# Reordering the first five microseconds of a convolution and ReGLU kernel: which queue fetches what, and in what order the band is built

## The chip, the cores and the metric

The kernel runs on one core of one Trainium2 chip. The metric is the device time of one execution in microseconds (us), with the median of several runs as the kernel's time. Five engines work side by side, each through its own queue of instructions in order: TensorE (PE in the profile; PEld is its weight load), VectorE (DVE), ScalarE (ACT), GpSimd (POOL) and SyncE (SP), which here only issues transfers.

## The reference

A causal convolution of seven taps along the sequence, one softmax-normalised set of taps for each of eight heads, followed by a feed-forward layer with a ReLU gate:

```python
# x: (8, 4096, 192), weight: (8, 7); 24 channels per head
w = softmax(weight, axis=-1)
x_pad = concat([zeros(8, 6, 192), x], axis=1)
conv[b, s, h, g] = sum_k w[h, k] * x_pad[b, s + k, h, g]
t = conv.reshape(32768, 192)
out = (maximum(t @ w_gate, 0) * (t @ w_val)) @ w_out   # 192 -> 1536 -> 192, float32
```

## The kernel before

The eight sequences are taken as two streams of four, `st` 0 and 1, which sit on the two halves of the partitions. The work goes in units of 1024 tokens of both streams, and a unit in two windows of 512. For a window, `gate_val` (L515) multiplies the convolved tokens `xc` with the gate and value weights, in twelve slices of 128 hidden columns; ScalarE applies the ReLU (L526), VectorE multiplies (L527). After two windows `project` multiplies with `w_out` (L544) and the results go out. There are sixteen units, and in each but the last, which ends a little differently, TensorE does the same 288 matmuls of L515 and 384 narrower ones of L544.

From the second unit on, the convolution is done on VectorE, ScalarE and GpSimd, one unit ahead, beside TensorE's work. The first unit has nobody ahead of it, so TensorE does its convolution itself, as a matmul with a band matrix: `band(h)` holds the seven taps of head h along its diagonals, and `conv_dense` (L366) multiplies 110 rows of x, each row a token, with it. That gives `xc` with channels on partitions, as L515 wants it. `conv_dense(0, c)` does it for each of three groups of 64 channels, c = 0, 1, 2, forty matmuls each, over five blocks `jj` of 104 tokens and the two streams. c = 0 uses heads 0, 1 and 2; c = 1 uses heads 2 to 5, and c = 2 heads 5 to 7.

The start, up to the first L515, is this:

- **x.** SyncE fetches blocks 1 to 4 of the first stream as fp32 into `room` (L120), and block 0 of both streams (L136); ScalarE casts the former to fp16 (L312), VectorE the latter (L327). Blocks 1 to 4 of the second stream are fetched by GpSimd's queue (L125), which casts on the way, straight to `x_h`. The small tensor `weight` goes first on SyncE's queue (L99).
- **The taps.** VectorE takes the maximum of the taps (L247), ScalarE exponentiates them (L250), VectorE sums, takes the reciprocal and scales (L254 to L257). A small matmul (L268) brings the taps of all heads to the partitions where they are wanted, in `spread`.
- **The mask and the band.** GpSimd writes a mask `spaced` (L126); VectorE sums it over the taps in two ways (L234, called twice), for `same` and `places`. The product of `spread` and `same` (L278) is `diag`; fourteen matmuls (L288) shift it into place in PSUM, seven for heads 0 to 3 (`bps`), seven for heads 4 to 7 (`spread`, second bank). Copies (L321) bring the band to fp16: VectorE heads 0 to 2, later head 3; ScalarE heads 4 to 7.
- **The weights.** GpSimd's queue fetches gate and value weights in slices (L168). Each is doubled to the upper partitions (L175); VectorE does so for the first two slices.
- **Warm-up.** `warm_up` (L152) issues matmuls on constants whose results nobody reads, in four places.

The order on each engine is the program's order, written out by hand; waits between engines are added from the data that instructions share. In `conv_dense(0, 0)` the blocks 1 to 4 of the first stream come first, then those of the second, and block 0 last:

```python
late = (1, 2, 3, 4, 0)
both = [(jj, (0, 1)) for jj in late]
if g == 0 and c == 0:
    both = [(jj, (st,)) for st in range(2) for jj in late[0:4]] + both[4:]
```

Of the kernel before, what the change touches and what calls it, by code (L numbers as in the profile page):

```python
# [8 lines left out]
FP = mybir.dt.float32  # L9
F16 = mybir.dt.float16  # L10
ACTF = mybir.ActivationFunctionType
ALU = mybir.AluOpType
# [3 lines left out]
def kernel(  # L16
# [12 lines left out]
    nc = tc.nc  # L29

    B, S, D = x.shape
    H, KW = weight.shape
    G = D // H
    DFF = moe_w_gate.shape[1]
    PAD = KW - 1
    NB = B // 2
# [5 lines left out]
    SUB = 112  # L42
    VECTOR = [(0, 5), (1, 5), (2, 5), (0, 6), (2, 1)]
    FOR_POOL = [(1, 6), (2, 6)]
    GSUB = 5
    DSUB = 104
# [12 lines left out]
    const = ctx.enter_context(tc.tile_pool(name="const", bufs=1))  # L59
# [33 lines left out]
    xts = {}  # L93
    ROWS0 = DSUB + PAD
    GAP = 12
    SEG = 16
    NSEG = SUB // SEG
    wr = const.tile([H, KW], FP)
    nc.sync.dma_start(out=wr[:], in_=weight)  # L99
    room = apool.tile([128, KW, NCH, LPOOL], FP, name="prods")  # L100

    def stage(p0, rows, st, n_st, jj, n):
        at = room[p0 : p0 + rows, 0, 0, 0:1]
        dims = [[D * GSUB, n_st], [D, n], [1, D]]
        return bass.AP(
            tensor=at.tensor,
            offset=at.offset + D * (GSUB * st + jj),
            ap=[at.ap[0]] + [d for d in dims if d[1] > 1],
        )

    xts[0] = xpool.tile([128, GSUB, 2, D], F16, name="x_h")

    def body(st):
        return bass.AP(
            tensor=x.tensor,
            offset=x.offset + (NB * st * S + DSUB - PAD) * D,
            ap=[[D, SUB], [DSUB * D, GSUB - 1], [1, D]],
        )

    nc.sync.dma_start(out=stage(0, SUB, 0, 1, 1, GSUB - 1), in_=body(0))  # L120
    ones = const.tile([128, SUB], FP)
    nc.vector.memset(ones[:], 1.0)
    spaced = const.tile([SUB, KW, SEG + 2 * GAP], FP)
    nc.gpsimd.memset(spaced[:], 0.0)
    nc.gpsimd.dma_start(out=xts[0][0:SUB, 1:GSUB, 1, :], in_=body(1))  # L125
    nc.gpsimd.affine_select(  # L126
        out=spaced[:, :, GAP : GAP + SEG],
        in_=ones[0:SUB, 0 : KW * SEG].rearrange("p (k s) -> p k s", k=KW),
# [3 lines left out]
        base=0,  # L132
        channel_multiplier=1,
    )
    nc.vector.memset(stage(0, 32, 0, 2, 0, 1), 0.0)
    nc.sync.dma_start(  # L136
        out=stage(PAD, DSUB, 0, 2, 0, 1),
        in_=bass.AP(
            tensor=x.tensor, offset=x.offset, ap=[[D, DSUB], [NB * S * D, 2], [1, D]]
        ),  # L140
# [4 lines left out]
    places = const.tile([SUB, 2 * SUB], F16)  # L145
# [4 lines left out]
    def warm_up(*widths):  # L150
        for n, w in enumerate(widths):
            nc.tensor.matmul(  # L152
                out=warm[:, n % 2, 0:w], lhsT=busy[:, 0:128], rhs=busy[:, 0:w], start=True, stop=True
            )

    warm_up(512, 512, 512, 512, 512, 512, 128)

# [13 lines left out]
    def both_halves(copy, s, dst):  # L173
        cols = slice(CUTS[s], CUTS[s + 1])
        copy(out=dst[64:128, :, cols], in_=dst[0:64, :, cols])  # L175
# [56 lines left out]
    def summed(out, step, n, at):  # L232
        with nc.allow_low_precision("one of the terms is not zero"):
            nc.vector.tensor_reduce(  # L234
                out=out,
                in_=bass.AP(
                    tensor=some.tensor,
                    offset=some.offset + at,
                    ap=[some.ap[0], [1, n], [step, KW]],
                ),  # L240
                axis=mybir.AxisListType.X,
                op=ALU.add,
            )

    pitch_k = SEG + 2 * GAP
    mx = const.tile([H, 1], FP)
    nc.vector.tensor_reduce(  # L247
        out=mx[:], in_=wr[:], axis=mybir.AxisListType.X, op=ALU.max, negate=True
# [9 lines left out]
        out=over[:],  # L258
        in0=spaced[0:H, 0, GAP : GAP + H],
# [1 line left out]
        scalar2=None,  # L261
        op0=ALU.mult,
    )
    same = const.tile([SUB, SEG], FP)
    summed(same[:], pitch_k, SEG, GAP)
    summed(places[:, SUB - SEG : SUB - SEG + SEG + KW - 1], pitch_k - 1, SEG + KW - 1, GAP)
    spread = psum.tile([128, 2, 512], FP, name="ps")
    nc.tensor.matmul(  # L268
        out=spread[0:SUB, 0, 0:H],
# [2 lines left out]
        start=True,  # L272
        stop=True,
    )
    warm_up(512)
    diag = const.tile([SUB, H, SEG], F16)
    with nc.allow_low_precision("products with one and zero"):
        nc.vector.tensor_tensor(  # L278
            out=diag[:],
            in0=spread[0:SUB, 0, 0:H].unsqueeze(2).to_broadcast([SUB, H, SEG]),  # L280
            in1=same[:].unsqueeze(1).to_broadcast([SUB, H, SEG]),
            op=ALU.mult,
        )
    bps = psum.tile([128, 2, 512], FP, name="ps")
    HB = H // 2
    for a in range(2):
        for b in range(NSEG):
            nc.tensor.matmul(  # L288
                out=(bps, spread)[a][:, a, HB * SEG * b : HB * SEG * (b + 1)],
                lhsT=places[:, SUB - SEG * (b + 1) : SUB - SEG * (b + 1) + 128],  # L290
                rhs=diag[:, HB * a : HB * (a + 1), :].rearrange("p h s -> p (h s)"),
                start=True,
# [1 line left out]
                skip_group_check=True,  # L294
            )

    warm_up(512, 128)

    taps = const.tile([H, KW], FP)
    nc.scalar.activation(taps[:], ex[:, 0:KW, 0], ACTF.Copy, scale=sm[:])  # L300
# [1 line left out]
    for h in range(H):  # L302
        r = G * h
        while r < G * (h + 1):
            c, n = r // 64, min(64 - r % 64, G * (h + 1) - r)
            nc.sync.dma_start(
                out=tap[r % 64 : r % 64 + n, c, :],
                in_=taps[h : h + 1, :].unsqueeze(1).to_broadcast([1, n, KW]),
            )
            r += n  # L310

    nc.scalar.copy(out=xts[0][0:ROWS0, 1:GSUB, 0, :], in_=stage(0, ROWS0, 0, 1, 1, GSUB - 1))  # L312
    bands = {}

    def fill_band(a, heads, copy):
        lo, n = heads[0] - HB * a, len(heads)
        part = const.tile([128, n, SUB], F16, name=f"band{heads[0]}")
        for i, h in enumerate(heads):
            bands[h] = part[0 : SUB + PAD, i, :]
        from_ = (bps, spread)[a][:, a, 0 : HB * SUB]  # L320
        copy(  # L321
            out=part[:].rearrange("p h (b s) -> p h b s", s=SEG),
            in_=from_.rearrange("p (b h s) -> p h b s", h=HB, s=SEG)[:, lo : lo + n],
        )

    fill_band(0, [0, 1, 2], nc.vector.tensor_copy)
    nc.vector.tensor_copy(out=xts[0][0:ROWS0, 0, :, :], in_=stage(0, ROWS0, 0, 2, 0, 1))  # L327
    fill_band(0, [3], nc.vector.tensor_copy)
    fill_band(1, [4, 5, 6, 7], nc.scalar.copy)

    def band(h):
        return bands[h]
# [8 lines left out]
    def conv_dense(g, c):  # L341


        xt = xts[g]
        if g == 0 and c == 0:
            xc[0] = xcpool.tile([128, NCH, UNIT], F16, name="xc")
            both_halves(nc.vector.tensor_copy, 0, Wg)
            both_halves(nc.vector.tensor_copy, 0, Wv)
        t0 = GROUPS[g][1][0]
        rows = ROWS0  # L350
        ps = psum.tile([128, 2, 512], FP, name="ps")
        late = (1, 2, 3, 4, 0)
        both = [(jj, (0, 1)) for jj in late]
        if g == 0 and c == 0:
            both = [(jj, (st,)) for st in range(2) for jj in late[0:4]] + both[4:]
        for jj, sts in both:
            col = DSUB * jj
            n = min(DSUB, WIN - col)
            for second in range(2):
                for st in sts:  # L360
                    for k2 in range(2):
                        k = 2 * c + k2
                        h0, h1 = 32 * k // G, (32 * k + 31) // G
                        h, m = (h0, G * h1 - 32 * k) if second else (h1, 32)
                        p0 = 64 * st + 32 * k2
                        nc.tensor.matmul(  # L366
                            out=ps[p0 : p0 + m, 0, col : col + n],
                            lhsT=xt[0:rows, jj, st, 32 * k : 32 * k + m],
                            rhs=band(h)[0:rows, 0:n],
                            start=True,  # L370
                            stop=True,
                            tile_position=(0, p0),
                            skip_group_check=True,
                        )
        copy = nc.vector.tensor_copy if c == 1 else nc.scalar.copy
        copy(out=xc[0][:, c, t0 : t0 + WIN], in_=ps[:, 0, :])
# [250 lines left out]
    for c in range(NCH):  # L627
        conv_dense(0, c)
# [81 lines left out]
```

## Time and profile before

| What | us |
|---|---|
| Median of 3 runs | 767.44 (767.3 to 769.09) |
| Profiled execution | 767.38 |
| Its span, first to last instruction | 765.40 |
| TensorE busy | 760.6 (99% of the span) |
| VectorE, ScalarE, GpSimd busy | 705.6, 600.8, 377.4 |
| First matmul of L366 | at 5.50 |
| First matmul of L515 | at 7.41 |

The span is what the trace shows; the execution's own time is 1.98 us longer. A line of the timeline gives the start in the span, the length from the first start to the last end, the engine, the line of the program, the operation, what it writes and reads, and how many instructions are merged into it; in brackets stands the idle time before it and what ended that. SPq and ACTq are transfers being issued by SyncE and ScalarE. A line of the windows gives, for a stretch, its length, busy time and number of instructions of PE, PEld, DVE, ACT and POOL, then the granted clock, the share of the DMA engines' time that was busy (overlapping packets can bring it over 1) and GB/s.

### The profile page before, as it was taken

To read this page: it belongs to the slowest core of one execution; us is meant where nothing else is said; L and a number is where in the kernel's file an instruction comes from. 1 tells how busy PE (TensorE), PEld (TensorE's weight loads), DVE (VectorE), ACT (ScalarE), POOL (GpSimd) and SP (SyncE) were. 2 spreads that over 40 slices of the span, in tenths; PEclk is the share of its full clock that TensorE was granted. 3 is DMA by queue.
4 is the path that set the end of the run, shared out by engine and by line. 5 is a ranking of instruction groups with operands and counts; after the bars stand their busy time and mean duration, and the time that the engine had idled before them with its cause. 6 is when DMAs were issued, how large, how long until landed. Compare 5 with 4: busy or idle time off the path is not lost.

```text
span 765.4 us, 25193 instructions
## 1 busy us (share of the span) xinstructions
PE 760.6 (99%) x10978; PEld 501.0 (65%) x10978; DVE 705.6 (92%) x763; ACT 600.8 (78%) x733; POOL 377.4 (49%) x242
## 2 busy tenths in 40 slices
PE   9999999999999999999999999999999999999998
PEld 4594674947649476584855848567494674947657
DVE  7998999999999999999999999999999999999891
ACT  6788887878878787887878878788787887875581
POOL 8419448093571926729175390853909347090000
PEclk9999999999999999999999999999999999999999
DMA  9979037290452805529173271823719034220202
GB/s 135 104 119 144 12 95 81 64 114 16 98 67 81 99 23 108 47 85 94 31 112 39 85 93 44 113 22 92 86 47 124 11 99 58 65 48 22 64 1 85
DMA packets 131396, 56.03 MB, mean 73 GB/s; under 512 B 96325, under 2 KB 131285, under 8 KB 131285
## 3 DMA queue, kind: packets, MB, share of 16 engines
q1 hardware_dynamic: 90661, 38.82, 24.0%
q0 software_dynamic: 40480, 15.50, 20.7%
q8 instruction: 86, 1.41, 0.8%
q14 instruction: 25, 0.20, 0.1%
q10 hardware_dynamic: 144, 0.10, 0.0%
HBM read 31.49 MB, written 25.17 MB: 74 GB/s over the span
## 4 chain that ended last, share of the span: by engine, by line
PE 99%; DMA 0%; ACT 0%; SPq 0%; issue 0%
PE ps L515 65%; PE ps L544 33%; PE ps L591 1%; PE ps L366 0%; DMA prods<-in_x_dram 0%; PE ps L387 0%; ACT x_h L312 0%; SPq L99 0%; ACT acc L570 0%
## 5 line engine op out<-in xcount | busy, mean ns | idle before, releaser
L527 DVE TENSOR_TENSOR hT<-gr,ps 128x1024 f16<-128x1024 f16 (+1 forms) x386 | 469.1, 1216 | 36.9 <-ACT gr L526 10.0
L526 ACT ACTIVATE gr<-ps 128x1024 f16<-128x1024 f32 (+1 forms) x386 | 393.3, 1020 | 102.0 <-PE ps L515 100.1
L467 POOL TENSOR_TENSOR prods<-prods 128x1344 f32<-128x1344 f32 x70 | 212.3, 3033 | 289.1 <-DVE prods L463 285.7
L515 PE MATMUL ps<-xc,Wg 64*128 64x512 f16 x2304 | 311.9, 376 | 0.0
L515 PE MATMUL ps<-xc,Wv 64*128 64x512 f16 x2304 | 311.9, 376 | 0.0
L544 PEld LDWEIGHTS <-hT 64*128 64x128 f16 x6048 | 249.8, 94 | 3.9 <-SPq L557 0.2
L544 PE MATMUL ps<-Wo,hT 64*128 64x192 f16 x6048 | 252.2, 243 | 0.0
L515 PEld LDWEIGHTS <-Wv 64*128 64x128 f16 x2304 | 129.7, 94 | 118.6 <-DVE hT L527 0.3
L515 PEld LDWEIGHTS <-Wg 64*128 64x128 f16 x2304 | 112.3, 94 | 132.4 <-issue 0.4
L489 DVE SCALAR_TENSOR_TENSOR acc<-x_r,tap,acc 128x576 f32<-128x576 f16 x225 | 165.4, 815 | 0.0
L461 ACT ACTIVATE prods<-x_r,tap 128x448 f32<-128x448 f16 x222 | 130.0, 659 | 3.1 <-DMA x_r<-x_p 3.1
L570 ACT COPY out_s<-ps 128x768 f32<-128x768 f32 (+1 forms) x63 | 45.1, 717 | 49.0 <-PE ps L544 40.4
L201 POOL DMA_DIRECT2D x_e<-in_x_dram x58 | 46.9, 817 | 17.1 <-ACT acc L477 13.8
L441 POOL COPY x_p<-x_e 128x960 f16<-128x960 f16 (+1 forms) x58 | 50.5, 913 | 2.0 <-DMA x_e<-in_x_dram 2.0
L467 POOL TENSOR_TENSOR xc<-prods 128x1344 f16<-128x1344 f32 x14 | 42.4, 3028 | 1.1
L489 DVE SCALAR_TENSOR_TENSOR xc<-x_r,tap,acc 128x576 f16<-128x576 f16 x45 | 34.1, 816 | 0.0
L477 ACT ACTIVATE acc<-x_r,tap 128x576 f32<-128x576 f16 x45 | 31.4, 765 | 0.1
L463 DVE TENSOR_SCALAR prods<-x_r,tap 128x448 f32<-128x448 f16 x70 | 26.7, 452 | 0.0
L570 DVE COPY out_s<-ps 128x384 f32<-128x384 f32 x16 | 8.9, 555 | 13.4 <-ACT out_s L570 13.4
L152 PE MATMUL ps<-const-bfloat16-1.0 128*128 128x512 bf16 (+1 forms) x10 | 3.7, 504 | 0.8 <-PEq L694 0.8
L366 PEld LDWEIGHTS <-x_h 110*32 110x32 f16 (+3 forms) x240 | 3.2, 92 | 2.0 <-issue 1.3
L366 PE MATMUL ps<-band,x_h 110*32 110x104 f16 (+7 forms) x240 | 3.9, 209 | 0.3 <-ACT x_h L312 0.3
(52 smaller groups left out, 55.5 us busy)
## 6 DMA issues: line engine op xcount, KB each, us to landing
out_dram<-out_s SPq DMA_DIRECT2D x63, 384.0 KB
x_e<-in_x_dram POOLq DMA_DIRECT2D x34, 192.0 KB, 7.0
x_e<-in_x_dram POOLq DMA_DIRECT2D x24, 240.0 KB, 5.4
x_r<-x_p SPq DMA_TRANSPOSE x131
Wo<-in_moe_w_out_dram POOLq DMA_DIRECT2D x1, 576.0 KB
x_h<-in_x_dram POOLq DMA_DIRECT2D x2, 210.0 KB, 5.4
x_h<-in_x_dram POOLq DMA_DIRECT2D x2, 192.0 KB, 4.1
prods<-in_x_dram SPq DMA_DIRECT2D x1, 336.0 KB
```

Source lines behind the costliest of these rows:

```text
L201: first = nc.gpsimd.dma_start(out=xe[:, j0 + start : j0 + n, st, :, :].rearrange("p j c r -> p j (c r)"), in_=bass.AP(tensor=x.tensor, off ...
L441: nc.gpsimd.tensor_copy(out=xp[:, j0 : j0 + n, :, st, :], in_=xe[:, j0 : j0 + n, st, :, :])
L461: engine.activation(out=out, in_=in_, func=ACTF.Copy, scale=scale)
L463: engine.tensor_scalar(out=out, in0=in_, scalar1=scale, scalar2=None, op0=ALU.mult)
L467: nc.gpsimd.tensor_tensor(out=pr[:, 0] if k < KW - 1 else xc[v + 1][:, :, LDVE:UNIT], in0=pr[:, 0], in1=pr[:, k], op=ALU.add,)
L477: last = nc.scalar.activation(out=accs[v][:, c, :], in_=shifted(v, c, 0, 0), func=ACTF.Copy, scale=tap[:, c, 0:1],)
L489: nc.vector.scalar_tensor_tensor(out=xc[v][:, c, 0:LDVE] if k == KW - 1 else acc[:, c, :], in0=shifted(v, c, k, 0), scalar=tap[:, c, k : k ...
L515: nc.tensor.matmul(out=pss[i][:, st, :], lhsT=W[64 * st : 64 * st + 64, c, 128 * f : 128 * (f + 1)], rhs=xcb[64 * st : 64 * st + 64, c, WI ...
L526: nc.scalar.activation(out=gr[:, sts], in_=pss[0][:, sts], func=ACTF.Relu)
L527: nc.vector.tensor_tensor(out=h[:, f, sts], in0=gr[:, sts], in1=pss[1][:, sts], op=ALU.mult)
L544: mm = nc.tensor.matmul(out=outs[q], lhsT=h[64 * r : 64 * r + 64, f, st, 128 * q : 128 * (q + 1)], rhs=Wo[64 * r : 64 * r + 64, f, :], sta ...
L570: one(out=dst[:, step * j : step * j + step], in_=src[:, step * j : step * j + step])
```

## The change

- `weight` is fetched by ScalarE's queue, ahead of its first activation; SyncE's first transfer is x.
- Of the second stream's blocks 1 to 4, SyncE fetches 1 and 2 as fp32, as its second transfer, and ScalarE casts them; GpSimd's queue fetches 3 and 4, now behind the mask.
- The two sums of the mask stand ahead of the taps' maximum on VectorE.
- `diag` is made in two halves, one per bank of the band.
- The band is copied in other pieces: block 0 is cast first on VectorE, then heads 0 and 1 are copied by VectorE, heads 2 and 3 and heads 4 to 7 by ScalarE.
- `conv_dense(0, 0)` takes both streams of a block together, as the other two do.
- The warm-up matmuls have other widths: the last of the first seven 256 columns instead of 128, 256 instead of 512 behind L268, 384 in one instead of 640 in two behind L288.

```diff
-    nc.sync.dma_start(out=wr[:], in_=weight)
+    nc.scalar.dma_start(out=wr[:], in_=weight)
...
-    def body(st):
+    def body(st, jj, n):
         return bass.AP(
             tensor=x.tensor,
-            offset=x.offset + (NB * st * S + DSUB - PAD) * D,
-            ap=[[D, SUB], [DSUB * D, GSUB - 1], [1, D]],
+            offset=x.offset + (NB * st * S + DSUB * jj - PAD) * D,
+            ap=[[D, SUB], [DSUB * D, n], [1, D]],
         )
 
-    nc.sync.dma_start(out=stage(0, SUB, 0, 1, 1, GSUB - 1), in_=body(0))
+    nc.sync.dma_start(out=stage(0, SUB, 0, 1, 1, GSUB - 1), in_=body(0, 1, GSUB - 1))
+    nc.sync.dma_start(out=stage(0, SUB, 1, 1, 1, 2), in_=body(1, 1, 2))
     ones = const.tile([128, SUB], FP)
     nc.vector.memset(ones[:], 1.0)
     spaced = const.tile([SUB, KW, SEG + 2 * GAP], FP)
     nc.gpsimd.memset(spaced[:], 0.0)
-    nc.gpsimd.dma_start(out=xts[0][0:SUB, 1:GSUB, 1, :], in_=body(1))
     nc.gpsimd.affine_select(
...
     )
+    nc.gpsimd.dma_start(out=xts[0][0:SUB, 3:GSUB, 1, :], in_=body(1, 3, 2))
...
-    warm_up(512, 512, 512, 512, 512, 512, 128)
+    warm_up(512, 512, 512, 512, 512, 512, 256)
...
     pitch_k = SEG + 2 * GAP
+    same = const.tile([SUB, SEG], FP)
+    summed(same[:], pitch_k, SEG, GAP)
+    summed(places[:, SUB - SEG : SUB - SEG + SEG + KW - 1], pitch_k - 1, SEG + KW - 1, GAP)
     mx = const.tile([H, 1], FP)
...
-    same = const.tile([SUB, SEG], FP)
-    summed(same[:], pitch_k, SEG, GAP)
-    summed(places[:, SUB - SEG : SUB - SEG + SEG + KW - 1], pitch_k - 1, SEG + KW - 1, GAP)
...
-    warm_up(512)
+    warm_up(256)
+    HB = H // 2
     diag = const.tile([SUB, H, SEG], F16)
     with nc.allow_low_precision("products with one and zero"):
-        nc.vector.tensor_tensor(
-            out=diag[:],
-            in0=spread[0:SUB, 0, 0:H].unsqueeze(2).to_broadcast([SUB, H, SEG]),
-            in1=same[:].unsqueeze(1).to_broadcast([SUB, H, SEG]),
-            op=ALU.mult,
-        )
+        for a in range(2):
+            nc.vector.tensor_tensor(
+                out=diag[:, HB * a : HB * (a + 1)],
+                in0=spread[0:SUB, 0, HB * a : HB * (a + 1)].unsqueeze(2).to_broadcast([SUB, HB, SEG]),
+                in1=same[:].unsqueeze(1).to_broadcast([SUB, HB, SEG]),
+                op=ALU.mult,
+            )
     bps = psum.tile([128, 2, 512], FP, name="ps")
-    HB = H // 2
...
-    warm_up(512, 128)
+    warm_up(384)
...
     nc.scalar.copy(out=xts[0][0:ROWS0, 1:GSUB, 0, :], in_=stage(0, ROWS0, 0, 1, 1, GSUB - 1))
+    nc.scalar.copy(out=xts[0][0:ROWS0, 1:3, 1, :], in_=stage(0, ROWS0, 1, 1, 1, 2))
...
-    fill_band(0, [0, 1, 2], nc.vector.tensor_copy)
     nc.vector.tensor_copy(out=xts[0][0:ROWS0, 0, :, :], in_=stage(0, ROWS0, 0, 2, 0, 1))
-    fill_band(0, [3], nc.vector.tensor_copy)
+    fill_band(0, [0, 1], nc.vector.tensor_copy)
+    fill_band(0, [2, 3], nc.scalar.copy)
     fill_band(1, [4, 5, 6, 7], nc.scalar.copy)
...
         both = [(jj, (0, 1)) for jj in late]
-        if g == 0 and c == 0:
-            both = [(jj, (st,)) for st in range(2) for jj in late[0:4]] + both[4:]
         for jj, sts in both:
```

## The prediction

> **What bounds the kernel now.** I read the page first, then the chain in order of time, then the timeline of the first ten microseconds by engine, then windows of that stretch. The engine row says that TensorE has next to nothing left to give:
>
> ```profile
> PE 760.6 (99%) x10978; PEld 501.0 (65%) x10978; DVE 705.6 (92%) x763; ACT 600.8 (78%) x733; POOL 377.4 (49%) x242
> ```
>
> The chain that ended last says where the rest is (start, length, what held it):
>
> ```profile
> 0.81 0.41 SPq L99
> 1.22 0.06 issue
> 1.28 3.31 DMA prods<-in_x_dram
> 4.59 0.02 issue
> 4.62 0.84 ACT x_h L312
> 5.46 0.04 issue
> 5.50 1.98 PE ps L366 x119
> 7.48 6.76 PE ps L515 x60
> ```
>
> After 5.50 us the chain lies on TensorE to the end, stage after stage of equal length. So everything this change can do is done by moving the moment at which the dense projections (L515) run freely; all behind it moves along unchanged. The page's clock column grants 1.0 throughout; what it does not show is told under the third rival.
>
> The timeline shows what prepares that moment (start, length, engine, line):
>
> ```profile
> 1.28 0.34 SPq L120 DMA_DIRECT2D prods<-in_x_dram  x1
> 1.67 0.46 SPq L136 DMA_DIRECT2D prods<-in_x_dram  x1
> ...
> 4.75 0.51 DVE L321 CAST band<-ps 128x336 f16<-128x336 f32 x1 [0.46 <-PE ps L288]
> 5.37 0.36 DVE L327 CAST x_h<-prods 110x384 f16<-110x384 f32 x1
> 5.65 0.27 DVE L321 CAST band<-ps 128x112 f16<-128x112 f32 x1
> ...
> 5.36 0.53 ACT L321 CAST band<-ps 128x448 f16<-128x448 f32 x1
> ...
> 14.17 0.64 PE L366 MATMUL ps<-band,x_h 110*32 110x104 f16 x40
> 14.73 0.82 PE L515 MATMUL ps<-xc,Wg 64*128 64x512 f16 x6
> ```
>
> The reader is to see three things. The first band of three heads is ready at 5.26, before x is. VectorE then stands idle until 5.37, with only L327 in its queue, whose input is SyncE's second x transfer (L136, block 0): that one lands at about 5.35. And 40 convolution matmuls that wait for nothing take 0.56 us (14.17 to 14.73).
>
> **What it removes.** The taps leave SyncE's queue, so x is issued at 0.81 instead of 1.28: 0.47 earlier, and ScalarE's cast can start at 4.15 and end at 4.98 at the old transfer rate.
>
> **What it adds on ScalarE.** An issue ahead of the table load. The only such issue in the trace (the last transfer, on ScalarE's queue) takes 0.37, so the exponentials start near 2.75 instead of 2.37, and all up to the small matmuls is 0.4 later. Against that stand VectorE's two mask sums, 0.35 and 0.42 at 3.39 and 3.67, which now run ahead of the taps: GpSimd can build the mask at about 1.4 instead of 2.40, since the 0.88 issue that was ahead of it goes behind. The bank of heads 0 to 3 was ready at 4.75, 0.73 behind the start of the product L278. That product started at 4.02; it would start near 4.4 and, in two halves, give the bank near 5.1. Its only reader on VectorE is now free no earlier than that (below), so this is costed at nothing; the cover is some 0.3, and beyond that it costs one for one. It is also no gain.
>
> **What it moves: block 0 and the band.** Before, the first matmul needed the band of heads 0 to 2, copied before block 0 was cast. Now VectorE casts block 0 first, then copies heads 0 and 1, then ScalarE copies heads 2 and 3. As built, this last copy (it reads the same PSUM bank) waits for VectorE's copy; the convolution's first matmul needs heads 0 and 1, its second needs head 2. So block 0, which was wanted last, now holds up the second matmul: landing L, +0.02, cast until the next copy may start 0.28 (5.37 to 5.65), a copy of 224 columns 0.39 (half way between 0.27 for 112 and 0.51 for 336), a hand-over of 0.03, ScalarE's 224 columns 0.32 (0.53 for 448, 0.59 for 512 at the same slope), 0.04 to the matmul. The sum is L + 1.08.
>
> The rival path on ScalarE is: cast to 4.98, the new cast of 384 columns some 0.45 (0.84 for 768, with a part that does not shrink), 0.32, 0.04, so 5.8. It loses if L is over 4.7.
>
> **When block 0 lands.** It is still issued near 1.67, but as SyncE's third transfer, behind 336 KB and the new 168 KB, 676 kB with its own 156 KB against 504 kB before. What the chip moved then:
>
> ```profile
> 2.00:3.00 1.00, 1.00 (x4) 0.35 (x3) 0.32 (x3) 0.68 (x3) 0.91 (x3) 1.00 0.31 48
> 3.00:4.00 1.00, 1.00 (x6) 0.45 (x4) 0.88 (x4) 0.30 (x1) 1.00 (x3) 1.00 1.05 345
> 4.00:5.00 1.00, 0.94 (x17) 0.60 (x16) 0.55 (x3) 0.38 (x1) 1.00 (x2) 1.00 1.41 231
> ```
>
> (The last column is GB/s, which is kB per us.) By 4.0 some 393 kB were in; the first transfer's 344 kB were in at 3.86 and its reader started at 4.62, so about 0.75 passes between last byte and use. With the same curve 0.47 earlier, 393 kB are in at 3.53. The remaining 283 kB take 0.82 at 345, or 1.23 at the 231 of the stretch that GpSimd's transfer shared: last byte at 4.35 or 4.76, L at 5.1 or 5.5. GpSimd's transfer starts later and is halved, so I stay nearer the first: L = 5.2. Bounds: as long from issue as the first transfer took (3.31 from 1.67), 4.98; 5.7 if the half moved to SyncE costs its whole time at the shared rate. So the matmuls run from 6.28 (6.06 to 6.78), not 5.50.
>
> **What comes back.** Before, they did not run freely: the first stream's blocks ran alone, then the second stream's had to land from GpSimd's queue, so 120 took from 5.50 to 7.41, 1.91. In the new order both streams go together, at 3 x 0.56 = 1.68. The first twelve projection matmuls took 1.44 (7.41 to 8.85) against 1.30 for twelve later (0.65 for six), since the copies of the convolution came late; with the even order they come in time. So the free run starts at 6.28 + 1.68 + 1.30 = 9.26 instead of 8.85: 0.41 later (0.2 to 0.9). The even point is a start at 5.87.
>
> **The rest, at nothing.** ScalarE's band of heads 4 to 7 (0.53) follows the other copy and is needed 0.56 after the second matmul: cover 0.1. GpSimd's halved x transfer, issued near 1.75, lands by 6.15 if it takes the old 4.4 and is wanted 0.28 into the run, at 6.56; cover 0.4. The weights move up in GpSimd's queue by 0 to 0.3; VectorE doubles their first part after the copy, near 5.9 instead of 6.15, and it is wanted at 8. The warm-up matmuls (128 columns more, then 256 and 256 fewer) stand in time in which TensorE waits anyway. SyncE's ten tap issues end near 11; GpSimd reads the taps at 23.46.
>
> **Sum.** The profiled execution took 767.38 (span 765.40 and 1.98 around it), 0.06 below the median of 767.44. 767.38 + 0.41 = 767.8. About 0.3% of it, 2.3 us, is what a measurement can tell from no change; the whole part of the kernel that is rearranged lasts 5.5 us, so this effect lies well below.
>
> **Rivals.**
> 1. *Block 0 comes early.* If SyncE's queue runs at its best rate all along and L is below 4.7, ScalarE's own 5.8 decides, or a little less: the run starts 0.1 to 0.3 earlier than the even point, 767.1 to 767.3. For it: 0.47 less to the first byte, and less from GpSimd in the way. Against it: the transfers' bytes grow by a third ahead of block 0. Chance 0.2.
> 2. *The halved transfer or the taps come late.* The second stream's last two blocks, now behind the mask on GpSimd, land after 6.56, or the taps after 2.5; each costs one for one beyond its cover. With up to 1 us more: 768.1 to 768.8. The trace gives no reason for it. Chance 0.1.
> 3. *TensorE's clock falls back* (slower). The seven warm-up matmuls of 3200 columns at the start take 2.83 us, 0.88 ns a column; in L515, a pair of 512 columns goes by in 0.216, 0.42 ns. So the chip starts at half speed and is at full speed by the convolution. The change leaves TensorE idle for about 0.9 before the convolution instead of 0.32. If that sent the clock back, a stretch like the first, 2.83 of half speed in the dense part, would cost 1.4, on top of 0.41: 769.2; two stretches, 770.6, past the bound. It decides once the idle time is long enough; at 0.32 it was not. Nothing in the trace says that 0.9 is. Chance 0.1, half of it past the bound with what adds up.
>
> The Trainium skill ("TensorE: Matmul & The Clock Gate", section "HAM oscillation — how this bites in real kernels") holds that the clock drops only over idle gaps of more than about 3.4 us, by which the third rival would not occur; no row here shows a gap between 0.32 and that length. Its Part 1 has a free-running window of 3.4 us, so a fall-back would by it cost an estimated 1.7, and the total would be 769.5.
>
> **How the numbers follow.** The forecast has 0.6 (767.5 to 768.3), the rivals 0.2, 0.1 and 0.1. The low end takes in rival 1 and the spread of the runs, 766.9; the high end rival 2 and the cheaper form of rival 3, 769.3 (one of the three runs was at 769.09). Faster by over 0.3% would need 2.3 out of 5.5 us: 0.02. Slower by over 0.3% needs rival 3 twice, or with a late landing: 0.06. The rest, 0.92, is within 0.3%.
>
> **What would show it.** In the new profile: x cast by ScalarE near 4.15; VectorE's cast of block 0 near 5.2, released by its DMA, the band copies in a row behind it; the second convolution matmul near 6.3; projections from near 8.0, even from the first on. I am wrong if block 0 is cast before 4.7, if the convolution waits for GpSimd's transfer or the small matmuls, or if 512-column pairs take 0.43 anywhere after 9 us.

## The result: 0.3% slower, and most of it is TensorE's clock

| | before | after |
|---|---|---|
| Median of 14 runs each, us | 767.50 (767.09 to 769.44) | 770.03 (768.52 to 771.23) |
| Ratio | | 1.0030, 95% interval 1.0022 to 1.0038 |
| Profiled execution / its span, us | 767.38 / 765.40 | 768.93 / 767.2 |
| Convolution matmuls in a row from | 5.50 | 6.70 |
| 13th projection matmul (the free run) | 8.85 | 11.06 |

The change costs 2.5 us at the median. The profiled execution is one of its better ones, 1.55 us above that of before. Its chain in order of time (start, length, what held it; a line of the program has a number a few higher than before):

```profile
1.79 3.70 DMA prods<-in_x_dram
5.48 0.02 issue
5.51 0.47 DVE x_h L329
5.98 0.30 DVE band L324
6.28 0.02 issue
6.30 0.35 ACT band L324
6.66 0.04 issue
6.70 2.43 PE ps L367 x108
9.13 7.31 PE ps L516 x60
```

The order is the one forecast: block 0 (the transfer of L137, issued at 1.79), its cast, VectorE's copy, ScalarE's copy, the convolution. But 119 matmuls take from 6.70 to the first projection at 9.06, 2.36, where 1.68 was expected for all 120. Before, the projections began so:

```profile
7.41 0.39 PE L515 MATMUL ps<-xc,Wg 64*128 64x512 f16 x2
...
8.85 0.82 PE L515 MATMUL ps<-xc,Wg 64*128 64x512 f16 x6
```

TensorE's timeline of the changed kernel:

```profile
4.75 0.57 PE L290 MATMUL ps<-diag,places 112*128 112x64 f16 x14
5.15 0.33 PE L153 MATMUL ps<-const-bfloat16-1.0 128*128 128x384 bf16 x1
6.32 0.21 PE L367 MATMUL ps<-band,x_h 110*32 110x104 f16 x1 [0.84 <-DVE band L324]
6.70 2.43 PE L367 MATMUL ps<-band,x_h 110*32 110x104 f16 x119 [0.17 <-ACT band L324]
9.06 0.61 PE L516 MATMUL ps<-xc,Wg 64*128 64x512 f16 x2
9.46 0.64 PE L516 MATMUL ps<-xc,Wv 64*128 64x512 f16 x2
9.89 0.64 PE L516 MATMUL ps<-xc,Wg 64*128 64x512 f16 x2
...
10.85 0.38 PE L516 MATMUL ps<-xc,Wv 64*128 64x512 f16 x2
11.06 0.81 PE L516 MATMUL ps<-xc,Wg 64*128 64x512 f16 x6
```

Two things stand there. TensorE is idle for 0.84 ahead of the first convolution matmul, then for another 0.17. And pairs of 512 columns start 0.43 apart at 9.46 and 9.89, but 0.21 apart at 10.85 and 11.06: half speed, then full speed. The windows of the same execution show it in the granted clock, the third number from the end:

```profile
6.00:7.00 1.00, 0.51 (x29) 0.39 (x32) 0.75 (x3) 0.70 (x2) 1.00 (x2) 1.00 0.99 100
7.00:8.00 1.00, 1.00 (x71) 1.00 (x60) 0.00 (x0) 0.61 (x2) 1.00 (x2) 0.55 1.33 162
8.00:9.00 1.00, 1.00 (x54) 0.88 (x43) 0.69 (x1) 0.06 (x1) 1.00 (x3) 0.50 1.17 126
9.00:10.00 1.00, 1.00 (x13) 0.40 (x8) 0.97 (x3) 0.58 (x1) 0.96 (x2) 0.50 1.41 165
10.00:11.00 1.00, 1.00 (x10) 0.39 (x8) 0.44 (x1) 0.00 (x0) 1.00 (x3) 0.74 1.40 159
11.00:12.00 1.00, 1.00 (x14) 0.45 (x10) 0.32 (x1) 0.94 (x2) 1.00 (x2) 1.00 1.55 183
```

From 0.55 and 0.74, the stretch at half clock goes from 7.1 to about 10.5, 3.4 us. TensorE's busy time in as long a stretch just ahead of it, in the changed kernel:

```profile
3.69:7.10 3.41, 1.97 (x56) 1.44 (x59) 1.87 (x7) 2.31 (x5) 3.41 (x6) 1.00 1.19 161
```

and in the kernel before, whose clock stays up:

```profile
3.63:7.04 3.41, 3.04 (x118) 2.44 (x119) 2.28 (x8) 1.72 (x3) 3.41 (x6) 1.00 1.44 206
```

1.97 of 3.41 against 3.04. The sum of the changed execution, by the prediction's own terms (1.68 and 1.30 are forecasts, not measured here): at full clock the free run would have started at 6.70 + 1.68 + 1.30 = 9.68, 0.83 later than 8.85. It started at 11.06, another 1.38 later. The last copy of the kernel, on ScalarE, starts 2.06 later than before; the remaining 0.15 is given back where the first stage of L545 runs in 15.95 instead of 16.09. Before and after:

```profile
761.83 0.32 ACT acc L570
763.89 0.32 ACT acc L571
```

Behind that copy another 0.51 is given back: it is 5.04 to the end of the execution, where it was 5.55. Part of this lies outside the span: the execution is longer than its span by 1.70 to 1.83 in twelve of the changed kernel's fourteen runs, and by 1.96 to 2.15 in the 84 runs of the kernel before that stand beside the experiments. No experiment asks what makes it.

### The profile page after: what moved, and what is told of

Its sections match the earlier page's. It is cut to its first block, busy times and chain, and to the rows that moved or that the text cites. A ratio compares the mean times of both kernels' runs of the same rounds, so it can differ in the third digit from the quotient of the medians.

```text
span 767.2 us, 25191 instructions
## 1 busy us (share of the span) xinstructions
PE 761.6 (99%) x10977; PEld 501.8 (65%) x10977; DVE 705.6 (92%) x763; ACT 601.2 (78%) x735; POOL 376.8 (49%) x242
## 4 chain that ended last, share of the span: by engine, by line
PE 99%; DMA 0%; DVE 0%; ACT 0%; issue 0%
PE ps L516 65%; PE ps L545 33%; PE ps L367 1%; PE ps L592 1%; DMA prods<-in_x_dram 0%; PE ps L388 0%; DVE x_h L329 0%; DVE prods L136 0%; ACT band L324 0%; ACT acc L571 0%; DVE band L324 0%; DVE ones L123 0%; DVE ex L230 0%; DVE places L147 0%; DVE same L235 0%
## 5 line engine op out<-in xcount | busy, mean ns | idle before, releaser
L528 DVE TENSOR_TENSOR hT<-gr,ps 128x1024 f16<-128x1024 f16 (+1 forms) x386 | 468.8, 1215 | 37.7 <-ACT gr L527 10.5
L516 PE MATMUL ps<-xc,Wg 64*128 64x512 f16 x2304 | 312.3, 376 | 0.0
L516 PE MATMUL ps<-xc,Wv 64*128 64x512 f16 x2304 | 312.2, 376 | 0.0
L545 PEld LDWEIGHTS <-hT 64*128 64x128 f16 x6048 | 249.9, 94 | 3.7
L545 PE MATMUL ps<-Wo,hT 64*128 64x192 f16 x6048 | 252.1, 243 | 0.0
L516 PEld LDWEIGHTS <-Wv 64*128 64x128 f16 x2304 | 130.0, 94 | 118.9 <-issue 0.7
L516 PEld LDWEIGHTS <-Wg 64*128 64x128 f16 x2304 | 112.1, 94 | 132.5 <-issue 0.7
L176 POOL COPY Wg<-Wg 64x768 f16<-64x768 f16 (+1 forms) x4 | 3.6, 908 | 1.8 <-DMA Wg<-in_moe_w_gate_dram 1.8
```

Of the source, the lines that this page charges most:

```text
L516: nc.tensor.matmul(out=pss[i][:, st, :], lhsT=W[64 * st : 64 * st + 64, c, 128 * f : 128 * (f + 1)], rhs=xcb[64 * st : 64 * st + 64, c, WI ...
L528: nc.vector.tensor_tensor(out=h[:, f, sts], in0=gr[:, sts], in1=pss[1][:, sts], op=ALU.mult)
L545: mm = nc.tensor.matmul(out=outs[q], lhsT=h[64 * r : 64 * r + 64, f, st, 128 * q : 128 * (q + 1)], rhs=Wo[64 * r : 64 * r + 64, f, :], sta ...
```

## The experiments

Theory A: block 0 ahead of the band makes the start late, and TensorE has too little to do meanwhile, so the clock falls back or comes up late; the two add up. The rivals are that the late start alone does it, that the clock's drop was an accident of one profile, or that the moved transfers do it. The edits are to the changed kernel, except in e2, e5 and e9, which start from the kernel before. Ratios are to the kernel before, measured beside each run; its medians there were 767.9 (e0 to e3), 767.71 (e4 to e7) and 767.53 (e8 and e9). They are not exactly ratios of the two medians.

**e0_again.** The changed kernel, no edit.

> The changed kernel as it is, once more, beside the kernel before. Theory A (late start and clock): block 0 of x is cast at 5.5 us and the convolution runs from 6.7 us, which costs 0.8 us; behind that TensorE is at half clock for one stretch of 3.41 us somewhere between 5 and 11 us, which costs up to 1.7 us more. Where in the program this stretch falls differs from execution to execution, so the runs should spread over some 2 us, from 768.3 to 771, with a median 2 to 3 us above the kernel before. Theory B (late start alone): the runs lie close together and the half-clock stretch of the one profile was an accident; median near 768.3.

Median 769.89 (769.32 to 771.05, 10 runs), ratio 1.0025 (1.0016 to 1.0034). The loss is reproduced. This profile, 770.60, shows another form of it. TensorE's timeline:

```profile
10.83 0.63 PE L516 MATMUL ps<-xc,Wg 64*128 64x512 f16 x2
11.26 0.63 PE L516 MATMUL ps<-xc,Wv 64*128 64x512 f16 x2
11.68 0.63 PE L516 MATMUL ps<-xc,Wg 64*128 64x512 f16 x2
12.11 0.63 PE L516 MATMUL ps<-xc,Wv 64*128 64x512 f16 x2
12.54 0.94 PE L516 MATMUL ps<-xc,Wg 64*128 64x512 f16 x6
13.31 0.81 PE L516 MATMUL ps<-xc,Wv 64*128 64x512 f16 x6
13.96 0.81 PE L516 MATMUL ps<-xc,Wg 64*128 64x512 f16 x6
```

Pairs stand 0.43 apart until 12.54, and six matmuls 0.65 apart from 13.31: here the clock did not fall back, it did not come up before about 12.8. (The windows' clock column says 1.00 through all of it; the spacing of the matmuls is the better witness.) Block 0 landed at 6.2 here, not 5.5, so the second convolution matmul was at 7.32 instead of 6.70. The last copy starts at 765.46, 3.63 later than before.

**e1_filled.**

```diff
-    warm_up(256)
+    warm_up(512, 512)
...
-    warm_up(384)
+    warm_up(512, 512, 512, 512, 512)
```

> The changed kernel with more warm-up matmuls, and nothing else: 512 and 512 columns instead of 256 behind the small matmul, five of 512 instead of one of 384 behind the band matmuls, so that TensorE is busy until the band arrives. Theory A (late start and clock): the clock stays at 1.0 from 3.7 us on, the 1.7 us are gone and the late start of 0.8 us stays: 768.2, 1.5 to 2 us less than the changed kernel, and the runs lie as close together as those of the kernel before. Theory B (late start alone): the start is the same, so the time is that of the changed kernel, near 770.

Median 769.36 (768.54 to 770.37, 11 runs), ratio 1.0016 (1.0008 to 1.0025): a miss for both. The profile shows why it tells nothing apart: the clock was still at half when the fill came, and five matmuls then last beyond the arrival of the band.

```profile
6.12 2.32 PE L153 MATMUL ps<-const-bfloat16-1.0 128*128 128x512 bf16 x5
8.38 1.66 PE L367 MATMUL ps<-band,x_h 110*32 110x104 f16 x120
```

The convolution starts at 8.38, pushed back by its own fill, and then runs at full clock.

**e2_bare.** The kernel before, less warm-up:

```diff
-    warm_up(512)
...
-    warm_up(512, 128)
```

> The kernel before, without the warm-up matmuls of 512 columns behind the small matmul and of 512 and 128 behind the band matmuls; the order of everything else and the start at 5.5 us stay. Theory A (the clock falls when TensorE idles in the start): TensorE has as little to do between 3.6 and 5.5 us as in the changed kernel; if that alone is enough for the clock to fall back, one stretch at half clock costs 1.7 us, 769.1; if the earlier start of the convolution (5.5 instead of 6.7) keeps it up, nothing is lost in most runs, 767.5, but more runs than before are at 769. Theory B (the clock plays no part): 767.4 to 767.5 in all but a few runs.

Median 769.01 (767.48 to 769.62, 11 runs), ratio 1.0011 (1.0002 to 1.0020). With before's order, only taking warm-up away costs about 1 us, as theory A has it. Its windows (profiled execution, 769.44):

```profile
6.00:7.00 1.00, 0.64 (x31) 0.48 (x27) 0.21 (x2) 0.14 (x1) 1.00 (x2) 0.94 1.36 161
7.00:8.00 1.00, 1.00 (x58) 1.00 (x52) 0.56 (x2) 0.42 (x1) 1.00 (x2) 0.50 1.33 166
```

The clock falls shortly before 7. GpSimd's transfer landed late in this execution too (6.6; before, the matmuls that read it began at 5.9), so the 2.0 us of this one profile are not the clock's alone.

**e3_band_first.** One step of the change undone:

```diff
+    fill_band(0, [0, 1, 2], nc.vector.tensor_copy)
     nc.vector.tensor_copy(out=xts[0][0:ROWS0, 0, :, :], in_=stage(0, ROWS0, 0, 2, 0, 1))
-    fill_band(0, [0, 1], nc.vector.tensor_copy)
-    fill_band(0, [2, 3], nc.scalar.copy)
+    fill_band(0, [3], nc.vector.tensor_copy)
```

> The changed kernel with one step undone: VectorE copies the band of heads 0 to 2 first, then casts block 0, then copies head 3; ScalarE copies heads 4 to 7 alone. Queues, mask and warm-up stay as in the changed kernel. Theory A (block 0 ahead of the band is the cause of the late start, and the late start that of the clock): the convolution starts at about 5.6 us, when ScalarE has cast the blocks; TensorE idles 0.3 us less than a microsecond; the clock stays up; 767.1 to 767.4, the changed kernel's loss is gone. Theory B (the queues are the cause: x of both streams now shares SyncE's queue, GpSimd's is behind the mask): the convolution still waits for a transfer, start after 6.2 us, and the time stays over 769.

Median 768.55 (766.58 to 768.97, 11 runs), ratio 1.0005 (0.9996 to 1.0014). The profile (766.58, the best run) is as theory A has it:

```profile
5.27 0.51 DVE L324 CAST band<-ps 128x336 f16<-128x336 f32 x1 [0.32 <-PE ps L290]
5.28 0.33 PE L153 MATMUL ps<-const-bfloat16-1.0 128*128 128x384 bf16 x1
5.48 0.53 ACT L324 CAST band<-ps 128x448 f16<-128x448 f32 x1
5.70 0.35 DVE L330 CAST x_h<-prods 110x384 f16<-110x384 f32 x1
5.83 1.54 PE L367 MATMUL ps<-band,x_h 110*32 110x104 f16 x120 [0.23 <-DVE band L324]
```

The transfers are those of the change, and the convolution no longer waits for block 0. So the moved transfers alone do not make most of the loss. But only two of eleven runs were under 768, and the median missed my 767.1 to 767.4. That the clock came up late in the other nine is likely but not shown, as the one profile is of the best run; e6_band_first_filled shows another thing that can hold this order up.

**e4_widths.** The changed kernel with before's warm-up behind the small matmul and the band:

```diff
-    warm_up(256)
+    warm_up(512)
...
-    warm_up(384)
+    warm_up(512, 128)
```

> The changed kernel with the warm-up widths of before behind the small matmul (512) and behind the band matmuls (512 and 128); everything else as changed. Theory A (late start, and a clock that asks for some three quarters of a window of 3.41 us to be filled with streaming columns): the windows of the start lose 512 columns in the change, 0.43 us at half clock; giving them back brings the clock up a window earlier in part of the runs, so the median is 0.3 to 1.0 us below the changed kernel's 769.9, between 768.9 and 769.6, and the late start of 0.8 us stays. Theory B (warm-up only fills time in which TensorE waits, as the prediction had it): no difference, 769.9.

Median 769.32 (767.57 to 771.45, 11 runs), ratio 1.0021 (1.0012 to 1.0029): inside theory A's range, but the interval overlaps that of the changed kernel, so the 512 columns that the change took away in these two places are not shown to matter. In this profile (769.53) the clock came up at about 10.2.

**e5_block0_first.** One step of the change done alone, in the kernel before:

```diff
+    nc.vector.tensor_copy(out=xts[0][0:ROWS0, 0, :, :], in_=stage(0, ROWS0, 0, 2, 0, 1))
     fill_band(0, [0, 1, 2], nc.vector.tensor_copy)
-    nc.vector.tensor_copy(out=xts[0][0:ROWS0, 0, :, :], in_=stage(0, ROWS0, 0, 2, 0, 1))
```

> The kernel before with one step of the change alone: VectorE casts block 0 ahead of the band of heads 0 to 2. All transfers, the mask and the warm-up stay. Theory A (block 0 ahead of the band makes the late start): the first convolution matmul moves from 5.5 to 6.2 us (block 0 at 5.37, 0.28, the copy 0.51); the clock falls back or comes late in more runs than before; 0.6 us and up to half of another 1.7: 768.3 to 769.3. Theory B (the moved transfers make it): block 0 lands here as early as before, 767.5 to 768.1, the same as before within 0.2.

Median 768.07 (767.60 to 769.32, 11 runs), ratio 1.0005 (0.9997 to 1.0014): not told apart from no change, under theory A's range and just inside theory B's. Theory B's mechanism it does not show: in the profile the cast of block 0 starts at 5.75 and the convolution at 6.57, a microsecond later than before. The warm-up of before was left in place, and the loss stayed small. The order alone is not enough for 2.5 us.

**e6_band_first_filled.** e3_band_first, and

```diff
-    warm_up(512, 512, 512, 512, 512, 512, 256)
+    warm_up(512, 512, 512, 512, 512, 512, 512, 256)
...
-    warm_up(256)
+    warm_up(384)
```

> The changed kernel with the band copied first, as in e3_band_first, and warm-up added where TensorE waits even at half clock: 512 columns more at the very start (they end before the small matmul's operands come), 384 instead of 256 behind the small matmul. Theory A (start and clock are all there is): the convolution starts at 5.8 us as in e3_band_first, the clock is full by then or soon after in nearly all runs; median 766.6 to 767.2, under the kernel before, and the runs above 768 that e3_band_first has mostly go. Theory B (e3_band_first's two kinds of runs have another cause than the clock): the same two kinds in the same share, median 768.5.

Median 767.47 (766.75 to 768.61, 11 runs), ratio 0.9997 (0.9988 to 1.0006). Three of eleven runs are above 768, against nine of e3_band_first. That is what theory A had of them, though the median is 0.3 above its range. It is the fastest version here, 0.0028 (some 2.1 us) under e0_again by the ratios, but not told apart from the kernel before. Its profile (767.35) shows a wait that the clock has no part in: the convolution starts at 5.96 at full clock, and then waits for GpSimd's halved transfer.

```profile
1.79 4.62 DMA x_h<-in_x_dram
...
6.45 1.46 PE ps L367 x97
```

The free run starts at 9.25 here and at 8.62 in the profile of e3_band_first, where that transfer came in time; the executions are 0.77 apart.

**e7_block0_second.** SyncE's second and third transfers swapped:

```diff
-    nc.sync.dma_start(out=stage(0, SUB, 1, 1, 1, 2), in_=body(1, 1, 2))
...
     nc.sync.dma_start(
         out=stage(PAD, DSUB, 0, 2, 0, 1),
...
     )
+    nc.sync.dma_start(out=stage(0, SUB, 1, 1, 1, 2), in_=body(1, 1, 2))
```

> The changed kernel with SyncE's second and third transfers swapped: block 0 is issued ahead of the half of the second stream; everything else as changed. Theory A (block 0's landing sets the start, and it waits behind the bytes ahead of it): it lands at about 4.9 instead of 5.5 us, the half stream near 5.4; the first convolution matmul is at about 5.9 instead of 6.3 and the second at 6.3 instead of 6.7; the time falls by 0.3 to 0.6 from 769.9, more if the clock is then kept up in more runs. Theory B (the transfer is held by its late issue or by a latency of its own): block 0 lands at 5.3 or later, no gain over 0.2.

Median 770.21 (768.96 to 770.76, 7 runs), ratio 1.0032 (1.0021 to 1.0042). No gain; my 0.3 to 0.6 was a miss. Block 0's cast still starts at 5.50, and the half stream is then the late one:

```profile
5.50 0.49 DVE L329 CAST x_h<-prods 110x384 f16<-110x384 f32 x1 [0.49 <-DMA prods<-in_x_dram]
...
6.10 0.51 ACT L315 CAST x_h<-prods 110x384 f16<-110x384 f32 x1 [0.64 <-DMA prods<-in_x_dram]
```

ScalarE's copy of heads 2 and 3 stands behind that cast, so the second matmul is at 6.91. Both of theory B's figures held. Block 0 was issued at 1.48 instead of 1.79, with 168 KB fewer ahead of it, and landed no earlier; in this one profile its landing does not follow the bytes ahead of it.

**e8_late_but_filled.** The changed kernel, late start and all, with

```diff
-    warm_up(512, 512, 512, 512, 512, 512, 256)
+    warm_up(512, 512, 512, 512, 512, 512, 512, 256)
...
-    warm_up(256)
+    warm_up(384)
...
-    warm_up(384)
+    warm_up(512, 256)
```

> The changed kernel, its late start kept, with warm-up that fits into TensorE's waits even at half clock: 512 columns more at the very start, 384 instead of 256 behind the small matmul, 512 and 256 instead of 384 behind the band matmuls (0.64 us at half clock, over before the band arrives; the fill of e1_filled took 2.1 and pushed the convolution back). Theory A (late start and clock add up): what is left is the late start, 0.8 to 0.9 us: median 768.3 to 768.9, clear below the changed kernel's 769.9. Theory B (the start is late by more than that and the clock costs little): 769.5 or more.

Median 767.90 (767.22 to 772.14, 12 runs), ratio 1.0005 (0.9992 to 1.0017). This is the decisive one: with nothing but 1024 columns more of matmuls that compute nothing, four fifths of e0_again's loss are gone (1.0025 to 1.0005). The intervals of these two just touch; that of the changed kernel's first measurement (1.0022 to 1.0038) lies clear of this one. The start is as late as ever, and the clock is up (profiled execution, 767.91):

```profile
6.50 0.21 PE L367 MATMUL ps<-band,x_h 110*32 110x104 f16 x1 [0.45 <-DVE band L324]
6.87 1.58 PE L367 MATMUL ps<-band,x_h 110*32 110x104 f16 x119 [0.17 <-ACT band L324]
8.38 0.39 PE L516 MATMUL ps<-xc,Wg 64*128 64x512 f16 x2
...
9.69 0.82 PE L516 MATMUL ps<-xc,Wg 64*128 64x512 f16 x6
```

The free run starts at 9.69, 0.84 later than before, and that costs 0.69 at the last copy (762.52) and 0.53 in the execution: what the late start is worth alone, by this one profile. I had put the median at 768.3 to 768.9; it is less, since the late start costs less than its own length. The fill does not help in every execution: four of the twelve runs are above 768, and one, 772.14, is the slowest of all; what held them is not known.

**e9_no_warm_up.** The kernel before without any of its warm-up:

```diff
-    warm_up(512, 512, 512, 512, 512, 512, 128)
...
-    warm_up(512)
...
-    warm_up(512, 128)
```

> The kernel before without any warm-up matmul; nothing else moves. It prices the clock alone: TensorE's stream starts with the convolution near 5.7 us. Theory A (full clock comes at the end of the first window of 3.41 us that is some three quarters full): full clock comes between 8.3 and 11.7 us, so 1.3 to 3 us are lost: median 769.2 to 770.3, as much as the changed kernel or more, with the order of before. Theory B (the clock matters less than the order): under 768.5.

Median 768.96 (767.83 to 769.39, 11 runs), ratio 1.0009 (1.0000 to 1.0017); the median is 0.2 under theory A's range and above theory B's. In the profiled execution pairs of 512 columns are 0.43 apart until 10.37, so full clock comes five microseconds after TensorE's stream begins. Even so it is 1 us better than the changed kernel, which starts its convolution a microsecond later.

Four kernels that differ in order and fill, as ratios to the kernel before (e8 has 384 columns behind the band matmuls that e6 has not):

| | thin warm-up | filled |
|---|---|---|
| block 0 first (late start) | e0_again 1.0025 (1.0016 to 1.0034) | e8 1.0005 (0.9992 to 1.0017) |
| band first | e3 1.0005 (0.9996 to 1.0014) | e6 0.9997 (0.9988 to 1.0006) |

Each edit alone takes some four fifths of the loss away, within intervals of 0.0009 to 0.0013 either way. That is what one would see if both act through the same thing, how much TensorE streams in its first six microseconds; the table does not show it by itself.

## Why the prediction was wrong

**What held.** The bound: from the second unit on every stage of L516 and L545 has the length it had before (31.08 and 15.84), and the last copy moves with the free run, by 2.06 for 2.21. The path: block 0's landing, its cast, two copies in a row, the second matmul. The cover of the small matmuls, mask and taps held as well; the exponentials started at 2.84 instead of the 2.75 forecast, with 0.59 for ScalarE's first issue instead of 0.37. ScalarE's cast of x began at 4.32, not 4.15.

**What was mis-sized: the late start.** 0.41 forecast, with bounds of 0.2 and 0.9; 0.83 by the sum above. Block 0 landed at 5.49 instead of 5.2 and took 1.21 to the second matmul instead of 1.08 (its cast 0.47, not 0.36). SyncE issued it at 1.79, not 1.67, and its queue had moved the whole volume by about 4.8, the slower of the two cases worked out for it. That the landing follows the bytes at all is not borne out by e7_block0_second. In other executions block 0 was used at 5.8 or 6.2. The term of 1.68 for the 120 matmuls was too long: in e8_late_but_filled, at full clock, 1.51 pass from the second of them (6.87) to the first projection (8.38), and 1.31 to the free run. With these lengths the late start is 0.67 and the clock's part 1.54 instead of 1.38. And of 0.84 in e8_late_but_filled only 0.5 to 0.7 reached the end, which the prediction's "all behind it moves along unchanged" did not allow.

**The step that failed** is the clock: the sum keeps it at full speed all through the start, and puts the warm-up matmuls at nothing because they "stand in time in which TensorE waits anyway". The time is free, but what TensorE does in it bears on the clock. Here that cost a stretch at half clock, 1.38 by the prediction's own terms. From e0_again to e8_late_but_filled, 1024 columns of fill are worth 0.0020 of 767.5, some 1.5 us, nearly four times the forecast's whole sum. That is the price of a good fill under the late start, and not of the columns that the change took away: e4_widths gives 512 of those back and gains 0.0004, within the noise. How much of the loss is the thinner warm-up, and how much the microsecond of waiting added in the same place, stays open.

**The rival that came true** is the third, the clock falling back, which had a chance of 0.1. Its price for one stretch, 1.4, came close to the 1.38 (or 1.54) of the profiled execution, in part by luck: it was worked out for a stretch of 2.83, and this one lasted 3.4. I held against it that nothing in the trace showed that 0.9 of idle time is long enough. In the changed kernel the gap is 0.84, and the fall comes 0.8 behind its end, in the middle of the convolution; TensorE was busy for only 1.97 of the 3.41 us ahead of the fall. In e2_bare it was 1.82 of the same length, with no gap over 0.7. That speaks for the busy share of a stretch rather than the length of one gap, but does not decide it: no profile that kept full clock has a gap over 0.6. The rule of the Trainium skill that I set beside it ("TensorE: Matmul & The Clock Gate", section "HAM oscillation — how this bites in real kernels"), no idle gaps of more than about 3.4 us, would have kept the clock up, and is not borne out by these traces. The window of 3.4 us in Part 1 of the same page of the Trainium skill agrees with them: the half-clock stretch here is 3.4 us long. The other form, the clock coming up late (12.8 us in e0_again), I had not thought of. It is the dearer one in the profiles: 770.60 there, against 768.93.

**The first rival**, an early block 0, is ruled out by the landing at 5.49. **The second**, late taps or a late half transfer on GpSimd's queue, did not show in the changed kernel: its convolution waited for neither. With the earlier start of e6_band_first_filled the half transfer did come late.

**Open.** How full a stretch must be for the clock to come up or to stay. Busy time alone does not settle it: in e0_again TensorE was busy for 3.09 of the 3.41 us from 2.55 to 5.96, and the clock stayed at half long after. Open too is why a third of the runs of the kernel before and of e8, and a few of e6, lie above 768. That fits a clock stretch that lies differently against each execution, and transfers that land up to 0.7 us apart, but no profile caught such a run of the kernel before.

## What to carry to other kernels

Where TensorE is the bound, as here, the matmuls ahead of the first real one can decide the time even when they compute nothing: an edit that shortens them, or delays the first real matmul, is to be costed as a change of the clock too, and not only of the wait. Size the fill for half clock, so that it ends before the operands come; more than that pushes the real work back, as e1_filled did. The spacing of equal matmuls in the profile shows whether it was enough. And a step that used to be wanted last (block 0) should not be put ahead, on the same engine, of one that is wanted first.

## What was not expected of the hardware

The clock can fall back with no idle gap over 0.84 us, and then stays at half for 3.4 us, at a cost of some 1.4 to 1.5 us here. It can also stay low through a start that is mostly busy, until 12.8 us. Two profiles of the same program show the two forms, which would explain why the runs of the changed kernel spread over 2.7 us. In these profiles the granted-clock column shows only a clock that falls after it was up; a start at half clock reads 1.00 there (e0_again) and is seen in the spacing of equal matmuls (0.43 against 0.21 for 512 columns). The first transfer issued by ScalarE occupied it for 0.59 us in the changed kernel, against 0.39 for its last one.
